# First-batch values moved to SyncE's queue as fp32 and cast by GpSimd; bias factors from a tiny exponential and a bf16 one-hot product; first keys turned ahead of first queries

## The chip, the cores and the metric

The kernel runs on one core of one Trainium2 chip. The metric is device time in microseconds (us), median of several executions. A core has five engines that run their own instruction lists in order and wait for each other by semaphores: TensorE (PE; its weight loads are listed apart as PEld), VectorE (DVE), ScalarE (ACT), GpSimd (POOL) and SyncE (SP). Transfers are issued from SP, ACT or POOL, each with a queue of its own, and all queues are served by the same 16 DMA engines.

## The reference

```python
def _attn_ref(q, k, v, bias_table):            # q, k, v: [8, 8, 576, 64]; bias_table: [32, 8]
    scores = scale * np.matmul(q, k.transpose(0, 1, 3, 2))
    n = np.abs(pos[:, None] - pos[None, :])
    bucket = np.where(n < 16, n, large)         # large: log-spaced buckets 16..31, 31 from distance 128 on
    scores = scores + bias_table[bucket].transpose(2, 0, 1)[None]
    attn = softmax(scores)                      # max taken off, divided by the sum
    return np.matmul(attn, v)

def _moe_ref(x, w1, w2, w3, w_out):             # x: [4608, 512]; d_ff = 768
    h = np.maximum(np.maximum(x @ w1, x @ w2), x @ w3)
    return h @ w_out
```

The attention's output for all 8 batches and 8 heads, laid out as 4608 tokens of 512 columns, is the input of the second function.

## The kernel before

The batches are worked one after the other, each in four **head pairs** (`hp` 0 to 3). Scores are kept turned (keys on partitions), so that `e = exp(scale * scores)` on ACT is already the left operand of the product with the values. The value tile `vx` carries a column of ones after the 64 columns of each head, so the product `a` gives the sum of the exponentials too; `quotients` on DVE divides by it and writes `x_sb`. TensorE turns `x_sb` into `xT`, and the feed-forward products on `xT` (`ps`, later `psp`, `pso`) are fitted between the attention products of the next batch.

The bias is not added but multiplied: DVE multiplies `e` by factors exp(bias - bias of the last bucket). Only a band near the diagonal differs from 1. `spread_bias` makes the factors by distance: a one-hot table `pick` (buckets by distances, built on DVE from a GpSimd iota) times the bias table gives `spread`; ACT turns it into the row `w_sb`, which is written to DRAM (`w_dr`), and SP reads it back shifted by one element per partition as `hank` (`load_hank`). `bandt`, two GpSimd copies of parts of `hank`, is the band for the last 64 keys; `times_bandt` on DVE needs it, and the second half of each first-batch `attend` product needs what `times_bandt` writes.

Of 576 positions, 512 are four tiles of 128 (`KT`), and 64 are a tail with tiles of its own (`qtail`, `ktail`, `vt`), two heads side by side with zeros or ones written by `constants`.

The **order** on each engine is that of the code, as nearly all instructions go through `inorder`. The head of the program, which the change touches, runs so:

- Keys and the first queries of batch 0 are read as fp32 on the queues of ACT and SP into parts of `xT` that are not yet in use (`k32`, `q32`), and cast to bf16 on DVE and ACT (`cast_keys`, `act_copy`). The other queries, the tails and all first values are read by GpSimd's queue, which casts on the way: `vx[0]` by eight transfers of a head each (L306).
- TensorE works nine products on zeros (`warm`) until there is input, then `spread`, then `first_transposes(0)`: queries, then keys, which DVE copies out as `qT` and `kT`.
- A first loop over the head pairs makes half of the scores and exponentials of batch 0 (`visit`), turning the next pair's queries and keys beside it. Then `load_second()` is written, and a second loop makes the other half and the products with the values.
- GpSimd's list goes on, behind the value transfers, with the first weight `w_bf` (L1066, `load_w(0)`), and then with what `load_second` issues: first two heads of batch 1's keys and queries (L247), their tails, the second weight (`load_w(1)`), the two `bandt` copies (L356), the other heads, casts (`spread_packed(0)`), batch 1's values and the third weight.

Of the kernel before, what the change touches and what calls it, by code (L numbers as in the profile page):

```python
# [10 lines left out]
F32 = mybir.dt.float32  # L11
# [28 lines left out]
def kernel(  # L40
# [84 lines left out]
    def dve_copy(out_, in_):  # L125
        return inorder(nc.vector.tensor_copy(out_, in_))
# [7 lines left out]
    def constants(i):  # L134
        inorder(nc.vector.memset(ktail[i][:], 0.0))
        if i == 0:
            inorder(nc.vector.memset(qtail[i][64:, :, :], 0.0))
        inorder(nc.vector.memset(vt[i][:], 0.0))
        inorder(nc.vector.memset(vx[i][:, :, :, D:AW], 1.0))
        for par in range(2):  # L140
            inorder(nc.vector.memset(vt[i][64 * par : 64 * par + 64, :, par, D:AW], 1.0))
# [88 lines left out]
    def borrow(c, n):  # L230
        return xT[:, c, NTOK - 2 * n :].bitcast(F32)

    k32 = borrow(3, KT * H * D).rearrange("p (t h d) -> p t h d", t=KT, h=H)
    q32 = borrow(2, 2 * KT * D).rearrange("p (t h d) -> p t h d", t=2, h=KT)

    def load_32(src, h, dst, eng, nt=KT):
        inorder(eng.dma_start(out=dst[:, :, h, :], in_=main_part(src, 0)[:, 0:nt, h, :]))
# [22 lines left out]
    table = stage.tile([NB, H], F32, name="table")  # L260
    nc.gpsimd.dma_start(out=table[:], in_=bias_table)
    ident = const.tile([P, P], BF16, name="ident")
    make_identity(nc, ident[:])
    load_32(k, 0, k32, nc.scalar)
    load_32(k, 1, k32, nc.scalar)
    for h in range(2, KT):
        load_32(q, h, q32, nc.scalar, 2)
    nc.scalar.preload_act_table_set("natural_log_exp_and_others")
    for h in range(2):
        load_32(q, h, q32, nc.sync, 2)  # L270
    for h in range(2, H):
        load_32(k, h, k32, nc.sync)
# [6 lines left out]
    nc.gpsimd.iota(ids[:, 0:NW], pattern=[[1, NW]], base=0, channel_multiplier=0)  # L279
    nc.gpsimd.iota(ids[:, NW:], pattern=[[0, 1]], base=0, channel_multiplier=1)  # L280
    pick = xT[0:NB, 1, spare].bitcast(F32)
    zeros = xT[:, 1, NTOK - CH :]
    inorder(nc.vector.memset(zeros, 0.0))
    constants(0)
    inorder(nc.vector.memset(qtail[1][64:, :, :], 0.0))
    dve_copy(pick[:], ids[:])
    ranges = _bucket_ranges(S, NB, 128)
# [8 lines left out]
    inorder(nc.vector.tensor_scalar(
        out=pick[:, 0:NW], in0=pick[:, 0:NW], scalar1=pick[:, NW:], scalar2=None, op0=ALU.is_equal,
    ))
    constants(1)
    load_main(q, 0, KT, H, batch[0][0], 0, 2)  # L300
    load_tail(k, 0, 0, H, k_diag)
    load_main(q, 0, 0, H, batch[0][0], 2, KT)
    load_q_tail(0)
    load_tail(v, 0, 0, H, v_diag)
    for h in range(H):
        in_turn(0, nc.gpsimd.dma_start(out=vx[0][:, :, h, 0:D], in_=main_part(v, 0)[:, :, h, :]))  # L306
# [13 lines left out]
    on_zeros(warm[:, 0:CH], 9)  # L320

    act_copy(batch[0][0][:, 0:2, 0:2, :], q32[:, :, 0:2, :])
    w_sb = stage.tile([H, WL], BF16, name="w_sb")

    def spread_bias():
        spread = ps_a.tile([H, NW], F32, tag="a", name="spread")
        mm(spread[:], lhsT=table[:], rhs=pick[:, 0:NW])
        negc = stage.tile([H, 1], F32, name="negc")
        inorder(nc.vector.tensor_scalar(
            out=negc[:], in0=spread[:, HALF:], scalar1=-1.0, scalar2=None, op0=ALU.mult,  # L330
        ))
        for out_, in_ in ((w_sb[:, HALF:], spread[:]), (w_sb[:, 0:HALF], spread[:, HALF:0:-1])):
            inorder(nc.scalar.activation(out=out_, in_=in_, func=ACTF.Exp, bias=negc[:]))
        inorder(nc.scalar.dma_start(out=w_dr[:], in_=w_sb[:]))
# [413 lines left out]
    def first_transposes(hp):  # L748


        hs = slice(2 * hp, 2 * hp + 2)
        tp = ps_f.tile([P, 2 * CH], BF16, tag="ff", name="tp1")
        K, L = KT * P, KT * P + P
        tq = tp[:, L:] if hp else ps_f.tile([P, 2 * CH], BF16, tag="ff", name="tq1")
        for t in range(2):
            tr(tq[:, P * t : P * t + P], batch[0][0][:, t, hs, :].rearrange("p h d -> p (h d)"), ident[:])
        for t in range(KT):
            tr(tp[:, P * t : P * t + P], batch[0][1][:, t, hs, :].rearrange("p h d -> p (h d)"), ident[:])
        e = K if hp < 2 else L
        if e > K:  # L760
            tr(tp[:, K:L], ktail[0][:, hp, :], ident[:])
        dve_copy(qk[0][0][:, hp, 0:QS], tq[:, 0:QS])
        dve_copy(qk[0][1][:, hp, 0:e], tp[:, 0:e])
# [304 lines left out]
    load_w(0)  # L1068
    batch[1] = load_tiles()
# [30 lines left out]
    for hp in range(HP):  # L1100
# [330 lines left out]
```

## Time and profile before

| | |
|---|---|
| time, median of 3 runs (lowest, highest) | 307.15 us (306.98, 308.83) |
| span of the profiled execution, first to last instruction | 305.2 us |
| what the median has more than this span | 1.95 us |
| busy PE / PEld / DVE / ACT / POOL | 295.5 / 183.7 / 206.3 / 201.3 / 143.7 us |
| DMA | 40.51 MB, mean 133 GB/s |

The profiled execution's own device time is not listed, only its span; 1.95 us is taken for what lies around a span. All starts below are in us from the span's start. A row of the timeline has the start, the busy time of the merged instructions, engine and line, what is written and read with shapes, the count, and in brackets the idle time of that engine just before and what ended it. `SPq` and `ACTq` are DMA issues. A row of the chain of waits has start, length and what the end of the program depended on. A row of the DMA issues has the size and the median us from issue to landing.

### The profile page before, as it was taken

The numbers are of one execution on the slowest core, as the hardware profiler recorded it, in microseconds if no ns is written. First come the engines' busy times: TensorE is split into PE (matmuls) and PEld (weight loads), VectorE is DVE, ScalarE is ACT, GpSimd is POOL, SyncE is SP. The second block draws the span as 40 slices with busy tenths as digits, with TensorE's granted clock in tenths as the row PEclk, the third lists the DMA queues.
The fourth block names the chain that finished last, engine by engine and source line by source line (L and its number), as shares of the span: only waits on it lengthen the run. The fifth ranks groups of instructions, "written<-read, shape, count | busy, mean of one in ns | idle before, by whom it ended". The sixth has DMA issues, their size and how long they took to land.

```text
span 305.2 us, 11001 instructions
## 1 busy us (share of the span) xinstructions
PE 295.5 (97%) x4745; PEld 183.7 (60%) x4745; DVE 206.3 (68%) x455; ACT 201.3 (66%) x270; POOL 143.7 (47%) x199
## 2 busy tenths in 40 slices
PE   8789999999999999999999999999999999999995
PEld 2367877765656676567666766676667654444442
DVE  6489888777776677676777677767776765453552
ACT  3999988977786787768776877677777720222211
POOL 8989677725839746774676469462000000000000
PEclk9999999999999999999999999999999999999999
DMA  9999999999999999999999999999623013202003
GB/s 160 187 203 194 176 137 120 114 165 128 223 150 121 150 131 205 174 143 192 181 139 135 202 162 146 138 197 171 79 46 140 6 40 94 84 0 108 31 0 137
DMA packets 165776, 40.51 MB, mean 133 GB/s; under 512 B 154584, under 2 KB 161248, under 8 KB 165728
## 3 DMA queue, kind: packets, MB, share of 16 engines
q0 software_dynamic: 105664, 16.66, 95.5%
q1 hardware_dynamic: 58304, 22.69, 41.6%
q8 instruction: 37, 0.61, 0.8%
q10 hardware_dynamic: 1760, 0.47, 0.7%
q14 instruction: 11, 0.09, 0.1%
HBM read 35.39 MB, written 9.45 MB: 147 GB/s over the span
## 4 chain that ended last, share of the span: by engine, by line
PE 80%; ACT 7%; DMA 6%; DVE 3%; SPq 2%; issue 1%; DVEq 0%; ACTq 0%
PE psp L109 32%; PE ps L109 15%; PE a L109 12%; PE sc L109 8%; PE pso L109 6%; ACT e L827 5%; DMA kT<-ktail 5%; PE sct L109 2%; PE warm L109 1%; PE scq L109 1%; ACT el L827 1%; SPq L738 1%; SPq L731 1%; DVE e L807 1%; DMA out_dram<-osb 1%
## 5 line engine op out<-in xcount | busy, mean ns | idle before, releaser
L827 ACT ACTIVATE e<-sc 128x1024 bf16<-128x1024 f32 x128 | 129.0, 1026 | 29.3 <-PE sc L109 28.0
L109 PEld LDWEIGHTS <-w_bf 64*128 64x128 bf16 (+1 forms) x1112 | 75.8, 95 | 55.3 <-issue 1.9
L109 PE MATMUL psp<-xT,w_bf 64*128 64x512 bf16 x784 | 97.2, 376 | 0.0
L807 DVE TENSOR_TENSOR e<-e,hank 128x512 bf16<-128x512 bf16 (+2 forms) x120 | 56.1, 473 | 13.9 <-ACT e L827 13.2
L109 PE MATMUL ps<-xT,w_bf 128*128 128x512 bf16 (+1 forms) x328 | 59.1, 332 | 0.0
L109 PE MATMUL sc<-qT,kT 64*128 64x256 bf16 (+1 forms) x352 | 48.5, 319 | 2.3 <-ACT e L827 1.1
L109 PEld LDWEIGHTS <-kT 64*128 64x128 bf16 (+1 forms) x712 | 30.0, 94 | 24.8 <-issue 6.8
L109 PE MATMUL a<-vx,e 64*128 64x65 bf16 (+1 forms) x1664 | 44.9, 190 | 0.0
L199 POOL DMA_DIRECT2D k_sb<-in_k_dram x48 | 36.2, 764 | 17.8 <-DMA vx<-in_v_dram 7.8
L199 POOL DMA_DIRECT2D q_sb<-in_q_dram x48 | 36.4, 767 | 15.1 <-DMA vx<-in_v_dram 5.7
L109 PEld LDWEIGHTS <-e 64*128 64x128 bf16 (+1 forms) x1664 | 40.8, 95 | 4.3
L109 PEld LDWEIGHTS <-hT 64*128 64x128 bf16 (+1 forms) x462 | 28.3, 95 | 18.7 <-DVE hT L551 1.6
L167 POOL DMA_DIRECT2D vx<-in_v_dram x28 | 24.8, 893 | 19.5 <-PE a L109 5.4
L109 PE MATMUL psp<-wo_bf,hT 64*128 64x256 bf16 (+1 forms) x360 | 31.7, 305 | 0.0
L421 ACT ACTIVATE m<-ps 128x512 bf16<-128x512 f32 x14 | 8.4, 597 | 34.3 <-PE ps L109 34.3
L827 ACT ACTIVATE el<-sct 128x576 bf16<-128x576 f32 (+2 forms) x36 | 21.7, 605 | 14.0 <-PE sct L109 13.9
L109 PEld LDWEIGHTS <-el 64*128 64x128 bf16 (+1 forms) x676 | 26.4, 94 | 7.0 <-issue 4.4
L109 PE MATMUL a<-vt,el 64*128 64x65 bf16 (+1 forms) x260 | 29.5, 198 | 0.2 <-DVE m L511 0.2
L551 DVE TENSOR_TENSOR hT<-psp,m 128x1024 bf16<-128x1024 f32 (+1 forms) x20 | 18.7, 956 | 9.1 <-PE psp L109 9.1
L109 PE MATMUL pso<-wo_bf,hT 128*128 128x512 bf16 (+2 forms) x102 | 21.7, 366 | 0.0
L430 DVE TENSOR_TENSOR m<-ps,m 128x512 bf16<-128x512 f32 x14 | 9.7, 692 | 17.0 <-PE ps L109 17.0
L537 DVE TENSOR_TENSOR m<-psp,m 128x1024 bf16<-128x1024 f32 x15 | 18.4, 1225 | 3.3 <-PE psp L109 3.1
(82 smaller groups left out, 292.8 us busy)
## 6 DMA issues: line engine op xcount, KB each, us to landing
out_dram<-osb SPq DMA_DIRECT2D x35, 256.0 KB, 4.7
vx<-in_v_dram POOLq DMA_DIRECT2D x28, 128.0 KB, 6.7
q_sb<-in_q_dram POOLq DMA_DIRECT2D x50, 64.0 KB, 5.3
k_sb<-in_k_dram POOLq DMA_DIRECT2D x48, 64.0 KB, 5.3
w_bf<-in_moe_w_dram POOLq DMA_DIRECT2D x2, 512.0 KB, 8.5
xT<-in_k_dram SPq DMA_DIRECT2D x6, 128.0 KB, 4.5
hank<-w_dr SPq DMA_DIRECT2D x2, 384.0 KB, 5.7
w_bf<-in_moe_w_dram POOLq DMA_DIRECT2D x1, 768.0 KB, 8.1
```

The costliest lines, as they stand in the source:

```text
L109: made = inorder(nc.tensor.matmul(*args, **kw))
L167: in_turn(b, nc.gpsimd.dma_start(out=dst[:, t, h0:h1, :], in_=x[:, t, h0:h1, :]), P * (h1 - h0))
L199: in_turn(b, nc.gpsimd.dma_start(out=dst[:, g, :, par, :], in_=part), KT * P)
L421: nc.scalar.activation(out=st[fb]["m0"][:], in_=ps0, func=ACTF.Copy)
L430: inorder(nc.vector.tensor_tensor(out=m[:], in0=ps1, in1=st[fb]["m0"][:], op=ALU.max))
L537: return lambda: inorder(nc.vector.tensor_tensor(out=m[0][:], in0=ps1(), in1=m[0][:], op=ALU.max,))
L551: inorder(nc.vector.tensor_tensor(out=out_[:, i : i + n], in0=ps2()[:, i : i + n], in1=m[0][:, i : i + n], op=ALU.max,))
L731: inorder(nc.sync.dma_start_transpose(out=made[j][:, g, 0 : KT * P].rearrange("p (t n) -> p t n", t=KT), in_=batch[b][j][:, g].rearrange(" ...
L738: inorder(nc.sync.dma_start_transpose(out=made[j][:, :, KT * P : KT * P + n], in_=(qtail, ktail)[j][b % 2][0:n].rearrange("p h c -> p (h c)"),
L807: put(nc.vector.tensor_tensor(out=e4[:, t, :, lo:hi], in0=e4[:, t, :, lo:hi], in1=hank[:, 2 * hp : 2 * hp + 2, c0:c1][:, :, ::-1], op=ALU. ...
L827: made = nc.scalar.activation(out=out_, in_=in_, func=ACTF.Exp, scale=inv_sqrt_d)
```

## The change

- **Bias factors.** Instead of `spread` in fp32 followed by two exponentials with a bias `negc` over 8 x 256 and 8 x 255, the table is read twice (the second time the row of the last bucket on all 32 partitions, by ACT's queue), DVE takes the difference `less` (32 x 8), ACT makes its exponential `factor` in bf16 (32 x 8), TensorE multiplies with a bf16 one-hot `pick`, and ACT copies the product into `w_sb` twice.
- **Head of the program.** Head 0 of the keys goes to SP's queue; `q32` holds two heads instead of four, and heads 2 and 3 of the first queries come by GpSimd's queue with the others. The iotas stand ahead of all GpSimd transfers. Six products on zeros instead of nine. `constants(1)` is moved into the first loop. `first_transposes(0)` turns keys first, then `spread`, then queries.
- **Values.** `vx[0]` is read as fp32 on SP's queue into `v32` (a part of `xT` not yet in use), two heads ahead of the two `hank` transfers and six behind them, and cast by GpSimd in four instructions (`cast_values`), the first ahead of `load_w(0)`, three behind it.

```diff
     def constants(i):
-        inorder(nc.vector.memset(ktail[i][:], 0.0))
-        if i == 0:
-            inorder(nc.vector.memset(qtail[i][64:, :, :], 0.0))
+        if i:
+            inorder(nc.vector.memset(ktail[i][:], 0.0))
+        inorder(nc.vector.memset(qtail[i][64:, :, :], 0.0))
...
-    q32 = borrow(2, 2 * KT * D).rearrange("p (t h d) -> p t h d", t=2, h=KT)
+    q32 = borrow(2, 4 * D).rearrange("p (t h d) -> p t h d", t=2, h=2)
...
-    table = stage.tile([NB, H], F32, name="table")
-    nc.gpsimd.dma_start(out=table[:], in_=bias_table)
-    ident = const.tile([P, P], BF16, name="ident")
-    make_identity(nc, ident[:])
-    load_32(k, 0, k32, nc.scalar)
+    ranges = _bucket_ranges(S, NB, 128)
+    far = next(i for i, r in enumerate(ranges) if r and r[0] <= HALF < r[1])
+    table = stage.tile([NB, 2, H], F32, name="table")
+    load_32(k, 0, k32, nc.sync)
     load_32(k, 1, k32, nc.scalar)
-    for h in range(2, KT):
-        load_32(q, h, q32, nc.scalar, 2)
-    nc.scalar.preload_act_table_set("natural_log_exp_and_others")
+    last_row = bass.AP(tensor=bias_table.tensor, offset=bias_table.offset + far * H, ap=[[0, NB], [1, H]])
+    inorder(nc.scalar.dma_start(out=table[:, 0, :], in_=bias_table))
+    inorder(nc.scalar.dma_start(out=table[:, 1, :], in_=last_row))
     for h in range(2):
         load_32(q, h, q32, nc.sync, 2)
+    nc.scalar.preload_act_table_set("natural_log_exp_and_others")
     for h in range(2, H):
         load_32(k, h, k32, nc.sync)
...
+    load_main(q, 0, 2, H, batch[0][0], 0, 2)
+    ident = const.tile([P, P], BF16, name="ident")
+    make_identity(nc, ident[:])
+    bucket = xT[0:NB, 1, spare].bitcast(F32)
+    pick = xT[0:NB, 2, 0:NW]
...
-    constants(1)
-    load_main(q, 0, KT, H, batch[0][0], 0, 2)
+    constants(0)
+    less = stage.tile([NB, H], F32, name="less")
     load_tail(k, 0, 0, H, k_diag)
+    load_tail(v, 0, 0, H, v_diag)
     load_main(q, 0, 0, H, batch[0][0], 2, KT)
     load_q_tail(0)
-    load_tail(v, 0, 0, H, v_diag)
-    for h in range(H):
-        in_turn(0, nc.gpsimd.dma_start(out=vx[0][:, :, h, 0:D], in_=main_part(v, 0)[:, :, h, :]))
+    v32 = borrow(0, KT * H * D).rearrange("p (t h d) -> p t h d", t=KT, h=H)
+
+    def cast_values(hp):
+        h = slice(2 * hp, 2 * hp + 2)
+        inorder(nc.gpsimd.tensor_copy(vx[0][:, :, h, 0:D], v32[:, :, h, :]))
...
-    on_zeros(warm[:, 0:CH], 9)
+    on_zeros(warm[:, 0:CH], 6)
+
+    cast_keys(0)
+    inorder(nc.vector.tensor_tensor(out=less[:], in0=table[:, 0, :], in1=table[:, 1, :], op=ALU.subtract))
+    factor = stage.tile([NB, H], BF16, name="factor")
+    inorder(nc.scalar.activation(out=factor[:], in_=less[:], func=ACTF.Exp))
...
-        mm(spread[:], lhsT=table[:], rhs=pick[:, 0:NW])
-        negc = stage.tile([H, 1], F32, name="negc")
-        inorder(nc.vector.tensor_scalar(
-            out=negc[:], in0=spread[:, HALF:], scalar1=-1.0, scalar2=None, op0=ALU.mult,
-        ))
+        mm(spread[:], lhsT=factor[:], rhs=pick)
         for out_, in_ in ((w_sb[:, HALF:], spread[:]), (w_sb[:, 0:HALF], spread[:, HALF:0:-1])):
-            inorder(nc.scalar.activation(out=out_, in_=in_, func=ACTF.Exp, bias=negc[:]))
+            act_copy(out_, in_)
         inorder(nc.scalar.dma_start(out=w_dr[:], in_=w_sb[:]))
...
+        for step in (queries, keys, put_queries, put_keys) if hp else (keys, spread_bias, queries, put_keys, put_queries):
+            step()
...
-    cast_keys(0)
-    spread_bias()
     first_transposes(0)
     on_zeros(warm[:, 0:CH])
+    cast_keys(1)
+
+    def load_values(h0, h1):
+        for h in range(h0, h1):
+            inorder(nc.sync.dma_start(out=v32[:, :, h, :], in_=main_part(v, 0)[:, :, h, :]))
+
+    load_values(0, 2)
     for h0 in (0, KT):
         load_hank(h0, h0 + KT)
-    dve_copy(batch[0][0][:, 0:2, 2:KT, :], q32[:, :, 2:KT, :])
-    cast_keys(1)
+    load_values(2, H)
+    cast_values(0)
...
     load_w(0)
+    for hp in range(1, HP):
+        cast_values(hp)
...
         if hp + 2 < HP:
             cast_keys(hp + 2)
+        if hp == 0:
+            constants(1)
```

On **GpSimd**, between the last query transfers of batch 0 and the `bandt` copies, this stood before (in the list of instructions, `xT<-in_k_dram` and `xT<-in_q_dram` are batch 1's keys and queries, `qtail_98` and `ktail_100` its tails):

```order
L177 DMA qtail_97<-in_q_dram 64x8x64
L188 DMA vt_95<-in_v_dram 64x4x64 x2
L306 DMA vx_93<-in_v_dram 128x4x64 x8
L1066 DMA w_bf<-in_moe_w_dram 128x4x768
L247 DMA xT<-in_k_dram 128x2x256
L247 DMA xT<-in_q_dram 128x2x256
L177 DMA qtail_98<-in_q_dram 64x8x64
L188 DMA ktail_100<-in_k_dram 64x4x64 x2
L1066 DMA w_bf<-in_moe_w_dram 128x4x256
L1066 DMA w_bf<-in_moe_w_dram 128x4x512
L356 COPY bandt<-hank 64x768 x2
```

and this stands there now:

```order
L177 DMA qtail_97<-in_q_dram 64x8x64
L311 CAST vx_93<-xT 128x4x2x64
L1088 DMA w_bf<-in_moe_w_dram 128x4x768
L311 CAST vx_93<-xT 128x4x2x64 x3
L247 DMA xT<-in_k_dram 128x2x256
L247 DMA xT<-in_q_dram 128x2x256
L177 DMA qtail_98<-in_q_dram 64x8x64
L188 DMA ktail_100<-in_k_dram 64x4x64 x2
L1088 DMA w_bf<-in_moe_w_dram 128x4x256
L1088 DMA w_bf<-in_moe_w_dram 128x4x512
L362 COPY bandt<-hank 64x768 x2
```

Eight issues, which waited for nothing, are gone; four casts stand in the list, each behind the landing of two heads of values on SP's queue, and all of `load_second`, the `bandt` copies too, stands behind the last of them.

On **SP** at the start of the program, before:

```order
L237 DMA xT<-in_q_dram 128x2x64 x2
L237 DMA xT<-in_k_dram 128x4x64 x6
L340 DMA hank<-w_dr 128x4x384 x2
L731 DMA_TRANSPOSE qT<-q_sb 128x4x128
L731 DMA_TRANSPOSE kT<-k_sb 128x4x128
```

and now:

```order
L237 DMA xT<-in_k_dram 128x4x64
L237 DMA xT<-in_q_dram 128x2x64 x2
L237 DMA xT<-in_k_dram 128x4x64 x6
L1076 DMA xT<-in_v_dram 128x4x64 x2
L346 DMA hank<-w_dr 128x4x384 x2
L1076 DMA xT<-in_v_dram 128x4x64 x6
L737 DMA_TRANSPOSE qT<-q_sb 128x4x128
L737 DMA_TRANSPOSE kT<-k_sb 128x4x128
```

Six of the eight value transfers stand behind `hank`, which waits on SP until `w_dr` has been written.

On **ACT** before the first exponentials (`e<-sc`), before:

```order
L237 DMA xT<-in_k_dram 128x4x64 x2
L237 DMA xT<-in_q_dram 128x2x64 x2
L268 ACT_TABLE_LOAD
L123 ACTIVATE q_sb<-xT 128x2x128
L333 ACTIVATE w_sb<-spread,negc 8x256
L333 ACTIVATE w_sb<-spread,negc 8x255
L334 DMA w_dr<-w_sb 8x511
```

and now:

```order
L237 DMA xT<-in_k_dram 128x4x64
L266 DMA table<-in_bias_table_dram 32x8
L267 DMA table<-in_bias_table_dram 32x8
L270 ACT_TABLE_LOAD
L330 ACTIVATE factor<-less 32x8
L123 ACTIVATE q_sb<-xT 128x2x128
L123 ACTIVATE w_sb<-spread 8x256
L123 ACTIVATE w_sb<-spread 8x255
L340 DMA w_dr<-w_sb 8x511
```

The small exponential has come in ahead of the query cast, and the two large ones have become copies.

More of the change, by code (lines that the diff above doesn't have):

```diff
@@ L278 @@
     ids = xT[0:NB, 0, spare].bitcast(mybir.dt.int32)
-    nc.gpsimd.iota(ids[:, 0:NW], pattern=[[1, NW]], base=0, channel_multiplier=0)
-    nc.gpsimd.iota(ids[:, NW:], pattern=[[0, 1]], base=0, channel_multiplier=1)
-    pick = xT[0:NB, 1, spare].bitcast(F32)
+    inorder(nc.gpsimd.iota(ids[:, 0:NW], pattern=[[1, NW]], base=0, channel_multiplier=0))
+    inorder(nc.gpsimd.iota(ids[:, NW:], pattern=[[0, 1]], base=0, channel_multiplier=1))
+    load_main(q, 0, 2, H, batch[0][0], 0, 2)
[3 more added lines that the diff above has]
+    pick = xT[0:NB, 2, 0:NW]
     zeros = xT[:, 1, NTOK - CH :]
     inorder(nc.vector.memset(zeros, 0.0))
[L284 to L287, printed above, removed]
+    inorder(nc.vector.memset(ktail[0][:], 0.0))
+    dve_copy(bucket[:], ids[:])
     single = 0
@@ L294 @@
             assert hi <= P or vv == NB - 1
-            inorder(nc.vector.memset(pick[:, lo : min(hi, NW)], float(vv)))
+            inorder(nc.vector.memset(bucket[:, lo : min(hi, NW)], float(vv)))
     inorder(nc.vector.tensor_scalar(
-        out=pick[:, 0:NW], in0=pick[:, 0:NW], scalar1=pick[:, NW:], scalar2=None, op0=ALU.is_equal,
+        out=pick, in0=bucket[:, 0:NW], scalar1=bucket[:, NW:], scalar2=None, op0=ALU.is_equal,
     ))
-    constants(1)
-    load_main(q, 0, KT, H, batch[0][0], 0, 2)
+    constants(0)
+    less = stage.tile([NB, H], F32, name="less")
     load_tail(k, 0, 0, H, k_diag)
+    load_tail(v, 0, 0, H, v_diag)
     load_main(q, 0, 0, H, batch[0][0], 2, KT)
     load_q_tail(0)
-    load_tail(v, 0, 0, H, v_diag)
-    for h in range(H):
-        in_turn(0, nc.gpsimd.dma_start(out=vx[0][:, :, h, 0:D], in_=main_part(v, 0)[:, :, h, :]))
+    v32 = borrow(0, KT * H * D).rearrange("p (t h d) -> p t h d", t=KT, h=H)
+    def cast_values(hp):
+        h = slice(2 * hp, 2 * hp + 2)
+        inorder(nc.gpsimd.tensor_copy(vx[0][:, :, h, 0:D], v32[:, :, h, :]))
     def cast_keys(hp):
@@ L754, in first_transposes, with queries, keys, put_queries @@
         tq = tp[:, L:] if hp else ps_f.tile([P, 2 * CH], BF16, tag="ff", name="tq1")
[L755 to L758, printed above, removed]
         e = K if hp < 2 else L
[L760 to L763, printed above, removed]
+        def queries():
+            for t in range(2):
+                tr(tq[:, P * t : P * t + P], batch[0][0][:, t, hs, :].rearrange("p h d -> p (h d)"), ident[:])
+        def keys():
+            for t in range(KT):
+                tr(tp[:, P * t : P * t + P], batch[0][1][:, t, hs, :].rearrange("p h d -> p (h d)"), ident[:])
+            if e > K:
+                tr(tp[:, K:L], ktail[0][:, hp, :], ident[:])
+        def put_queries():
+            dve_copy(qk[0][0][:, hp, 0:QS], tq[:, 0:QS])
+        def put_keys():
+            dve_copy(qk[0][1][:, hp, 0:e], tp[:, 0:e])
+        for step in (queries, keys, put_queries, put_keys) if hp else (keys, spread_bias, queries, put_keys, put_queries):
+            step()
     def last_keys():
```

## The prediction

> **What bounds the kernel now.** I read the share of busy time first, then a table by stage, then the chain of waits through the first 32 us, since every edit lies there.
>
> ```profile
> PE 295.5 (97%) x4745; PEld 183.7 (60%) x4745; DVE 206.3 (68%) x455; ACT 201.3 (66%) x270; POOL 143.7 (47%) x199
> 8.00:16.00 8.00, 6.37 (x62) 2.87 (x60) 3.30 (x11) 7.59 (x11) 8.00 (x12) 1.00 1.69 194
> 16.00:24.00 8.00, 6.73 (x129) 4.89 (x126) 6.90 (x19) 7.63 (x13) 6.96 (x11) 1.00 1.60 191
> 24.00:32.00 8.00, 7.82 (x129) 6.13 (x126) 7.20 (x22) 7.62 (x15) 7.67 (x11) 1.00 1.44 197
> ```
>
> The last three rows are stages of 8 us: busy PE, PEld, DVE, ACT, POOL, the granted clock, the DMA share and GB/s. From 8 to 24 us ACT is full and PE is not. From 24 us on PE is full (7.82 of 8), and over the whole span it is busy 97%: nothing behind 24 us has room to win back what is lost ahead of it, and what is won ahead of it stays won, unless a wait there eats it. The DMA engines are never without work in these stages, and POOL has hardly an idle moment: it is the engine of the list of transfers.
>
> ```profile
> 7.81 1.95 ACT e L827 x2
> 12.65 1.83 ACT e L827 x2
> 22.34 0.60 PE a L109 x18
> 26.67 1.00 PE a L109 x27
> 27.67 0.87 PE ps L109 x8
> ```
>
> So says the chain of waits (its rows between 5 and 32 us, five of them): exponentials from 7.81 us, then products with the values, then the first feed-forward products. No DMA stands in this piece of it. The question is whether the change puts one there.
>
> **The head: what it gains.**
>
> ```profile
> 1.29 0.66 POOL L261 DMA_DIRECT2D table<-in_bias_table_dram  x1 [0.85 <-POOLq L1415]
> 1.19 4.02 PE L109 MATMUL warm<-xT 128*128 128x512 bf16 x9 [1.19 <-DVE xT L283]
> 2.92 0.28 DVE L126 CAST xT<-xT 32x257 f32<-32x257 int32 x1 [0.22 <-POOL xT L280]
> 3.72 0.34 DVE L296 TENSOR_SCALAR xT<-xT 32x256 f32<-32x256 f32 x1
> 4.21 0.42 ACT L123 ACTIVATE q_sb<-xT 128x256 bf16<-128x256 f32 x1
> 4.93 0.43 DVE L126 CAST k_sb<-xT 128x512 bf16<-128x512 f32 x1
> 5.14 1.02 PE L109 MATMUL spread<-xT,table 32*8 32x256 f32 x2
> 6.38 0.82 ACT L333 ACTIVATE w_sb<-spread,negc 8x256 bf16<-8x256 f32 x2 [1.75 <-DVE negc L329]
> 7.23 0.53 ACTq L334 DMA_DIRECT2D w_dr<-w_sb  x1
> 7.81 3.77 ACT L827 ACTIVATE e<-sc 128x1024 bf16<-128x1024 f32 x4 [0.61 <-PE sc L109]
> ```
>
> The one-hot table waits for GpSimd's iota. It loses the transfer of 0.66 ahead of it and `ident`'s two instructions between; I put its end about 1.0 earlier (at least 0.66), so the int cast starts near 1.88 instead of 2.92. From that cast to the end of the comparison are 1.14 us (2.92 to 4.06), then `constants(0)`, 0.9 us of memsets that stood ahead of it before. The first key cast so starts near 3.95 instead of 4.93 and ends at 4.4. The difference `less` behind it is priced like the smallest DVE rows, 0.15; the small exponential has no row (bounds 0.1 and 0.47, the larger being half the `w_sb` row); I take 0.3, ending near 4.9. ACT then works in a line: query cast 0.42, the two copies into `w_sb` 0.82 (bounds 0.6 and 0.9 for copies in place of exponentials), the issue 0.53. That ends at 6.8, and the first `e` starts near 6.85 instead of 7.81: **1.0 us earlier**, 0.5 if the second table transfer lands late. PE keeps up: its product on `factor` is one bf16 pass in place of the 1.02 us in fp32, the two query turns and their copy end near 6.05, scores near 6.7. The nine products take 4.02 us, six take 2.7, so they end at 3.9, ahead of the keys: nothing waits for them. `w_dr` goes out near 6.3 instead of 7.23. `constants(1)`, 0.9 us, now stands in the first loop where DVE is busy 3.30 of 8 us: hidden; uncovered it would cost 0.9. Heads 2 and 3 of the queries arrive by GpSimd's queue instead of ACT's; if they come late for the second pair's turn, up to 0.5 of the 1.0 goes.
>
> **The values: what they do to GpSimd's list.**
>
> ```profile
> 9.42 5.96 POOL L306 DMA_DIRECT2D vx<-in_v_dram  x8
> 16.04 0.77 POOL L247 DMA_DIRECT2D xT<-in_k_dram  x1
> 17.53 0.71 POOL L247 DMA_DIRECT2D xT<-in_q_dram  x1 [0.72 <-DMA vx<-in_v_dram]
> 18.27 0.70 POOL L177 DMA_DIRECT2D qtail<-in_q_dram  x1
> 18.96 1.25 POOL L188 DMA_DIRECT2D ktail<-in_k_dram  x2
> 20.18 1.52 POOL L1066 DMA_DIRECT2D w_bf<-in_moe_w_dram  x2
> 21.67 1.79 POOL L356 COPY bandt<-hank 64x768 bf16<-64x768 bf16 x2
> 25.47 0.89 POOL L252 COPY q_sb<-xT 128x512 bf16<-128x512 bf16 x1
> 23.92 0.25 DVE L907 TENSOR_TENSOR el<-el,bandt 128x192 bf16<-128x192 bf16 x1
> 24.25 0.22 PE L109 MATMUL a<-vt,el 128*128 128x130 bf16 x1
> ```
>
> Before, GpSimd only issues; it passes the values at 15.3 us although they have not landed, and `bandt` is ready at 23.46, 0.46 us ahead of the DVE product that reads it, behind which PE goes on at 24.25. Taking out 5.96 us of issues looks like a gain. But what stands in their place waits for landings, and all of `load_second` waits behind it. Call L the landing of the last value transfer. After it GpSimd does the last cast (0.8: no fp32 cast of this size is in the trace; two bf16 copies of it took 0.89 and 0.64, and 1.8 would be the two `bandt` copies), the same seven issues (0.77, and 4.14 from 17.53 to 21.67: 4.9), `bandt` (1.8), and 0.3 more bring DVE and PE to the place of 24.25. PE resumes there at L + 7.8, so the change costs **L - 16.45**, whatever the head has won. This wait stands on DVE, in front of all its later work: quotients, and so `x_sb`, its turns and the feed-forward products; ACT stops when its score banks are full. All that comes later is moved as a whole.
>
> **When the last value lands.**
>
> ```profile
> xT<-in_k_dram SPq DMA_DIRECT2D x6, 128.0 KB, 4.5
> hank<-w_dr SPq DMA_DIRECT2D x2, 384.0 KB, 5.7
> w_bf<-in_moe_w_dram POOLq DMA_DIRECT2D x1, 768.0 KB, 8.1
> SPq L340 <- DMA w_dr<-w_sb: 5.0, 1, 5.0
> 10.81 0.92 SPq L340 DMA_DIRECT2D hank<-w_dr  x2
> 2.50:5.00 2.50, 2.50 (x7) 0.70 (x5) 2.03 (x25) 1.70 (x2) 2.50 (x7) 1.00 1.17 244
> 17.00:17.75 0.75, 0.04 (x2) 0.06 (x1) 0.75 (x3) 0.75 (x2) 0.22 (x1) 1.00 2.36 157
> 19.50:21.50 2.00, 2.00 (x46) 1.58 (x45) 1.97 (x5) 1.88 (x3) 2.00 (x4) 1.00 1.16 209
> ```
>
> Three rows of issues (KB, us to landing), SP's wait for `w_dr`, the `hank` issue, and three stretches whose last number is GB/s: fp32 reads of batch 0, value reads alone, and the first weight nearly alone. `hank` went out 3.58 us after `w_dr` (7.23 to 10.81); from 6.3 that gives 9.9, and its second half lands near 10.3 + 5.7 = 16.0. SP issues the six values from 10.8 to 13.8, behind it on one queue. Values 0 and 1 go out by 6.7 and land near 11 (4.5), the first cast ends at 12, and the first weight is issued then, on the other queue, so it is in service before value 2. What is left at 16.0 is the weight, 786 KB at 209 GB/s = 3.8 us, and six values of 131 KB at 244 = 3.2 us. If the queues share, the last value is the last of this list: L = 16.0 + 7.0 = **23.0**, and the cost is **6.55 us**. Bounds: if SP's queue were served first, `hank`'s second half would land 5.0 (the shorter of its two) after 10.3, and the values 3.2 behind it: L = 18.5, cost 2.1. At the other end, the whole list ended before with the weight at 15.3 + 8.1 = 23.4; eight values now take 4.3 us at 244 GB/s instead of 3.3 (64 KB each at 157), so L = 24.4, cost 8.0.
>
> Do the queues share? `hank` and the values beside it say so:
>
> ```profile
> DMA to landing us min/median/max: 3.2/4.3/5.4
> DMA to landing us min/median/max: 5.4/5.9/6.3
> DMA to landing us min/median/max: 5.0/5.7/6.4
> ```
>
> These are values 0 and 1 (issued 9.42 and 10.16), values 1 and 2 (10.16 and 10.90), and the halves of `hank` (10.81, and about 0.4 later). Value 0, ahead of `hank`, took 3.2; value 1 landed at 15.5, with `hank`'s first half at 15.8, and value 2 at 17.2, its second half at 17.6 (6.4): one small transfer per large one, both slowed. The Trainium skill, "DMA: Bandwidth & Descriptors", section "Queues, rings and completion order", has each DMA engine take turns between queues packet by packet; by that rule the weight's few large pieces go out among the first values and the last value ends the list, as in the forecast, and the trace agrees (15.5 against 15.8). Strict order by queue would give the 2.1 us instead.
>
> The sum against the profiled execution: 305.2 + 6.55 = 311.7 us of span; with the median's 1.95 us more, **313.7 us**. The head's 1.0 us and the fewer products on zeros do not enter: they end in front of the wait.
>
> **Rivals.**
>
> *SP's queue gets ahead of the weight* (L from 18.5 to 21): cost 2.1 to 4.6, time 309.2 to 311.7. For it: GpSimd's transfers start later after their issue. Against: the pairs just shown.
>
> *GpSimd gets through in time.* The wait decides from L = 16.45 on; if the values land ahead of that, the head's gain is kept, 307.15 - 1.0 = 306.2, and the 5.96 us of issues that are gone may bring batch 1's loads forward. For it: GpSimd's list was 0.46 us ahead of DVE with the eight issues in it. Against: value 7 is issued only at 13.3, behind 786 KB of `hank`; this needs a landing within 3.1 us, the best value landing of before (3.2, with nothing large beside it).
>
> *TensorE slows down in the wait.* At the start, after standing still, nine 512-column products took 4.02 us, 0.45 each; `ps` in the chain takes 0.87 for eight of 256 columns, 0.22 per 512. So PE starts at half pace, for 4 us and more. If a stop of 6 us behind 24 us brings it back there, 4 to 5 us at half pace cost 2.0 to 2.5 where PE is full: 315.7 to 316.2. Against: between 8 us and the end the trace shows no slow pace, nor a stop of this length. The Trainium skill, "TensorE: Matmul & The Clock Gate", section "What's actually happening", says that the clock falls to half after an idle window of about 3.4 us and needs a busy one to return; by that rule this rival holds once the wait is over 3.4 us, and no trace here shows a fall.
>
> *The change does nothing where it counts*: the head's gain and a late `bandt` of a us cancel, within 1%.
>
> **How the numbers follow.** The forecast (shared queues, cost 5.5 to 7.5) 0.38; with the slow restart (7.5 to 10) 0.22; SP's queue ahead 0.20; within 1% or so by cancelling 0.09; in time, with the head's gain, 0.11. The likeliest gives 313.7. The first three make 0.80, from 309.0 to 317.2; about 1% (3 us) is what a measurement of this kernel can tell from no change. Slower by over that: 0.38 + 0.22 and most of SP's queue ahead, 0.72. Within: 0.22, among them most of the case in time, whose gain is only 1.0. Faster by over 1%: 0.06, if batch 1's earlier loads also pay.
>
> **What would show it.** Head: first `e` on ACT near 6.85. Values: GpSimd idle before the second cast until near 20 us, before the last until 23, on value landings; `bandt` near 29 to 31 instead of 21.67; on DVE an idle time of some 6 us before the `bandt` product, released by POOL; PE idle just before the product that follows it. I am wrong if the casts end by 16.5, if the weight lands well behind the values, or if DVE does not wait for `bandt`.

## The result and the profile after

| | before | after |
|---|---|---|
| time, median (lowest, highest), same chip | 307.34 us (306.98, 308.83), 4 runs | 316.48 us (316.05, 318.09), 4 runs |
| ratio, 95% interval | | 1.0286 (1.024 to 1.0332) |
| span of the profiled execution | 305.2 us | 315.1 us |

The change makes the kernel 9.1 us slower: slower as forecast, inside the range, and 2.8 us above the predicted 313.7. The share of busy time and the granted clock over the whole span, of the kernel after:

```profile
PE 298.9 (95%) x4741; PEld 185.7 (59%) x4741; DVE 205.1 (65%) x454; ACT 201.2 (64%) x271; POOL 139.5 (44%) x194
PEclk9999699999999999999999999999999999999999
```

PE is busy 3.4 us longer, for fewer products: part of them ran at a lower clock, which the fifth slice of the clock's row (6) shows, from 31.5 to 39.4 us. GpSimd has 4.2 us less to do than before, and this bought nothing.

The same stages of 8 us as before, of the kernel after (start:end, length, busy PE, PEld, DVE, ACT, POOL, granted clock, DMA share, GB/s):

```profile
24.00:32.00 8.00, 2.06 (x38) 1.32 (x36) 0.91 (x3) 2.72 (x5) 7.12 (x11) 0.93 0.77 77
32.00:40.00 8.00, 7.62 (x94) 5.82 (x95) 6.39 (x19) 4.82 (x10) 7.96 (x11) 0.65 1.48 190
40.00:48.00 8.00, 8.00 (x135) 6.67 (x134) 6.12 (x18) 7.54 (x15) 6.16 (x9) 1.00 1.86 178
```

From 24 to 32 us PE worked 2.06 us where it had worked 7.82 before: a hole. From 32 to 40 us it is busy again, but at a clock of 0.65, and gets through 94 products; one stage later it does 135 in the same time at full clock.

Who waited in the hole is told by the timelines. GpSimd, VectorE and TensorE of the kernel after:

```profile
15.09 0.61 POOL L311 CAST vx<-xT 128x512 bf16<-128x512 f32 x1 [6.43 <-DMA xT<-in_v_dram]
15.64 0.77 POOL L1088 DMA_DIRECT2D w_bf<-in_moe_w_dram  x1
18.60 0.71 POOL L311 CAST vx<-xT 128x512 bf16<-128x512 f32 x1 [2.19 <-DMA xT<-in_v_dram]
24.82 0.61 POOL L311 CAST vx<-xT 128x512 bf16<-128x512 f32 x1 [4.72 <-DMA xT<-in_v_dram]
30.20 1.78 POOL L362 COPY bandt<-hank 64x768 bf16<-64x768 bf16 x2
32.01 0.26 DVE L924 TENSOR_TENSOR el<-el,bandt 128x192 bf16<-128x192 bf16 x1 [7.10 <-POOL bandt L362]
32.33 0.29 PE L109 MATMUL a<-vt,el 128*128 128x130 bf16 x1 [4.82 <-DVE el L924]
```

Read from the bottom: PE stood still 4.82 us for the banded product; DVE stood still 7.10 us for `bandt`; the `bandt` copies start at 30.20 instead of 21.67, since GpSimd's list in front of them waited four times for values, the last time until 24.82. The product at 32.33 stood at 24.25 before: 8.08 us later. TensorE had already waited 1.46 us, until 25.48, for the last cast itself, since the products of the fourth head pair read those values; `bandt` was needed behind them.

The chain of waits of the kernel after carries it through SP's queue (start, length, what was waited for):

```profile
6.74 4.36 DMA w_dr<-w_sb
11.11 0.37 SPq L346
...
12.08 0.72 SPq L1076
...
17.15 7.55 DMA xT<-in_v_dram
...
25.42 1.41 POOL xT L247 x2
...
30.26 0.84 POOL bandt L362
31.15 0.83 POOL bandt L362
32.01 0.27 DVE el L924
32.33 1.28 PE a L109 x18
```

A transfer now stands in the piece of the chain where there was none: the last value, issued at 17.15, in which 7.55 us of waiting lie. In the prediction's terms it lands at L = 24.70.

Whether anything is lost or won later shows in the same exponential far apart. The pair that starts at 42.02 us after and at 32.06 before, and one near the end:

```profile
42.02 1.94 ACT L844 ACTIVATE e<-sc 128x1024 bf16<-128x1024 f32 x2 [0.44 <-PE sc L109]
253.03 1.02 ACT L844 ACTIVATE e<-sc 128x1024 bf16<-128x1024 f32 x1 [0.53 <-PE sc L109]
32.06 1.94 ACT L827 ACTIVATE e<-sc 128x1024 bf16<-128x1024 f32 x2 [0.44 <-PE sc L109]
243.11 1.03 ACT L827 ACTIVATE e<-sc 128x1024 bf16<-128x1024 f32 x1 [0.54 <-PE sc L109]
```

The first two rows are of after, the others of before. The distance is 9.96 us at the one place and 9.92 at the other, and the spans differ by 9.9. All of the loss arises ahead of 42 us, 8.1 in the wait and 1.9 between 32 and 42 us, and is then handed on.

### The profile page after: what moved, and what is told of

Read it like the earlier page. It is cut to its first block, busy times and chain, and to the rows that moved or that the text cites. A ratio compares the mean times of both kernels' runs of the same rounds, so it can differ in the third digit from the quotient of the medians.

```text
span 315.1 us, 10997 instructions
## 1 busy us (share of the span) xinstructions
PE 298.9 (95%) x4741; PEld 185.7 (59%) x4741; DVE 205.1 (65%) x454; ACT 201.2 (64%) x271; POOL 139.5 (44%) x194
## 4 chain that ended last, share of the span: by engine, by line
PE 82%; DMA 5%; ACT 4%; DVE 2%; POOL 2%; SPq 2%; issue 1%; ACTq 0%; POOLq 0%; DVEq 0%
PE psp L109 35%; PE ps L109 16%; PE a L109 13%; PE sc L109 8%; PE pso L109 6%; DMA xT<-in_v_dram 2%; PE sct L109 2%; ACT e L844 2%; SPq L1076 2%; DMA w_dr<-w_sb 1%; PE scq L109 1%; DMA table<-in_bias_table_dram 1%; ACT el L844 1%; DMA out_dram<-osb 1%; POOL bandt L362 1%
## 5 line engine op out<-in xcount | busy, mean ns | idle before, releaser
L109 PE MATMUL sc<-qT,kT 64*128 64x256 bf16 (+1 forms) x352 | 49.4, 329 | 1.2 <-ACT e L844 0.6
L109 PEld LDWEIGHTS <-e 64*128 64x128 bf16 (+1 forms) x1664 | 41.5, 95 | 5.8 <-issue 1.6
L109 PEld LDWEIGHTS <-el 64*128 64x128 bf16 (+1 forms) x676 | 27.1, 95 | 13.0 <-issue 5.4
L167 POOL DMA_DIRECT2D vx<-in_v_dram x28 | 24.8, 892 | 17.4 <-DMA vx<-in_v_dram 9.7
```

Of the source, the lines that this page charges most:

```text
L109: made = inorder(nc.tensor.matmul(*args, **kw))
L167: in_turn(b, nc.gpsimd.dma_start(out=dst[:, t, h0:h1, :], in_=x[:, t, h0:h1, :]), P * (h1 - h0))
```

## Experiments

All times are medians, with lowest and highest run in brackets. The kernel before ran on the same chip in each group: 307.19, 307.11 and 307.21 us in the three groups. Ratios are to these. They lie within 0.23 us of the 307.34 above, so a median is also compared with the changed kernel's 316.48 where the difference is much larger than that.

### One half of the change at a time

`head_alone` has the new bias factors and the new head, with the values by GpSimd's queue as before:

```diff
-    v32 = borrow(0, KT * H * D).rearrange("p (t h d) -> p t h d", t=KT, h=H)
...
+    for h in range(H):
+        in_turn(0, nc.gpsimd.dma_start(out=vx[0][:, :, h, 0:D], in_=main_part(v, 0)[:, :, h, :]))
...
```

> The changed kernel with its new head (bias factors, keys first, six products on zeros), but the first values read by GpSimd's queue as bf16, as before the change. Theory one (GpSimd's list waits for values and holds back the bandt copies): the wait on DVE ahead of the bandt product is gone, and the time is within 1% of before, 306.5 to 309.5 us, as the head's own gain is small. Rival (the head itself costs most, as the second pair's keys and the clock came late in it): 312 us or more.

Measured 309.16 us (308.38 to 310.06), ratio 1.0061 (1.0037 to 1.0085). `values_alone` is the kernel before with only the values changed (fp32 on SP's queue, four casts):

```diff
-    for h in range(H):
-        in_turn(0, nc.gpsimd.dma_start(out=vx[0][:, :, h, 0:D], in_=main_part(v, 0)[:, :, h, :]))
...
+    load_values(0, 2)
     for h0 in (0, KT):
         load_hank(h0, h0 + KT)
+    load_values(2, H)
...
```

> The kernel before with the values alone changed: fp32 on SP's queue, two heads ahead of hank and six behind, four GpSimd casts around the first weight. Theory one: nearly all of the loss is here, 314.5 to 317 us, bandt product on DVE at 31 to 33 us. Rival (the head costs most): 307 to 310 us.

Measured 315.84 us (314.69 to 317.33), ratio 1.0274 (1.021 to 1.0337). The wait is the same one, 5.2 us on DVE here. A row of its timeline and one of its waits (engine, line, what was waited for, us in total, times, longest):

```profile
23.19 0.61 POOL L309 CAST vx<-xT 128x512 bf16<-128x512 f32 x1 [4.74 <-DMA xT<-in_v_dram]
DVE el L910 <- POOL bandt L359: 5.2, 1, 5.2
```

So the values cost 8.6 us by themselves and the head 2.0; together they would give 10.6 where 9.1 were measured, so the two losses don't add by some 1.5 us. The head, which I had down for 1.0 us of gain, is a small loss. What became of its gain comes further down.

### What GpSimd's list has in front of the band

`casts_behind_bandt` takes the last three casts out of the way: they stand behind the `bandt` copies.

```diff
     load_w(0)
-    for hp in range(1, HP):
-        cast_values(hp)
...
                 make_bandt()
+                for hp in range(1, HP):
+                    cast_values(hp)
```

> The changed kernel with the three later value casts moved behind the two bandt copies in GpSimd's list; every transfer, its queue and its order on SP stay. Theory one: bandt is ready near 23, the products with the values wait instead for the casts (last one near 25.5 us), and the time falls to 309.5 to 312 us. Rival (the value traffic on SP's queue is what costs, wherever GpSimd waits for it): 315 to 317 us, as in the changed kernel.

Measured 312.37 us (311.92 to 313.23), ratio 1.0161 (1.0095 to 1.0227). The best of all orders with the new values, 4.1 us less than the changed kernel. GpSimd of this kernel, and the wait of TensorE:

```profile
21.86 1.82 POOL L362 COPY bandt<-hank 64x768 bf16<-64x768 bf16 x2
23.74 1.17 POOL L311 CAST vx<-xT 128x512 bf16<-128x512 f32 x2
27.81 0.61 POOL L311 CAST vx<-xT 128x512 bf16<-128x512 f32 x1 [2.90 <-DMA xT<-in_v_dram]
24.40 0.60 PE L109 MATMUL a<-vx,e 128*128 128x65 bf16 x8 [2.66 <-POOL vx L311]
```

`bandt` is back at its old time (21.67 before), so it was the landings in front of it that delayed it and not the copies. The time did not come back whole: TensorE now waits 2.66 us for the second cast, which waits for nothing but the `bandt` copies in front of it, and TensorE's clock was down behind this wait too (the last section has the row). The last value lands later still (27.7), presumably as more transfers stand beside it, but its cast is done by 28.4, just ahead of the first product that reads it (28.66). An order with the second and third cast ahead of `bandt` and only the last behind it wasn't tried. The expected 312 was missed by 0.4.

`weight_behind_casts` keeps the casts in front, and moves the first weight's transfer behind them, so that it can't stand beside the values:

```diff
-    load_w(0)
     for hp in range(1, HP):
         cast_values(hp)
+    load_w(0)
```

> The changed kernel with the first weight's transfer issued behind the last value cast instead of ahead of the second. Theory one with shared queues: values 6 and 7 no longer stand behind the weight's pieces and land near 19 instead of 24.3 and 24.7, bandt is ready near 27, the time is 309.5 to 312.5 us, and the weight lands near 25, in time for its first product. Rival (the last values are late because SP issues them late and hank is slow): they land at 23 or later and the time stays over 314 us.

Measured 314.28 us (313.33 to 316.83), ratio 1.0233 (1.0163 to 1.0304). Two rows of GpSimd:

```profile
21.67 0.61 POOL L311 CAST vx<-xT 128x512 bf16<-128x512 f32 x1 [1.56 <-DMA xT<-in_v_dram]
27.75 1.79 POOL L362 COPY bandt<-hank 64x768 bf16<-64x768 bf16 x2
```

The last cast starts 3.15 us earlier than in the changed kernel (24.82), so the weight did hold the last values. `bandt` starts 2.45 us earlier only: the weight's own issue, 0.77 us, now stands behind the last cast. The time is 2.2 us less. I had expected 309.5 to 312.5, with landings near 19: I had left out that issue and SP's slow issue of the last two values. The gain may be larger than it looks: the trace of this kernel has a wait of 1.65 us for turned keys at 119.69 us, like the one that comes up below for the head.

### What holds the last values beside the weight

In the changed kernel the value issued just ahead of the weight (at 14.94) landed 4.4 us later; the one issued just behind it (15.93) took 8.3, and so did the weight itself (15.64). These are the rows for these single issues of the changed kernel, in this order (us to landing last), and below them the one for a value that was issued at 15.65 in `weight_behind_casts`, with no weight beside it:

```profile
xT<-in_v_dram SPq DMA_DIRECT2D x1, 128.0 KB, 4.4
DMA to landing us min/median/max: 8.3/8.3/8.3
w_bf<-in_moe_w_dram POOLq DMA_DIRECT2D x1, 768.0 KB, 8.3
DMA to landing us min/median/max: 4.2/4.2/4.2
```

So it is the weight, and not the place on SP's queue, that makes 8.3 us of 4.2. Is it the size of the weight's pieces (its writes are of 1536 bytes)? `weight_in_thirds` loads it as three transfers:

```diff
-        for f0, f1 in ((0, QS), (QS, d_ff)) if i else ((0, d_ff),):
+        for f0, f1 in ((0, QS), (QS, d_ff)) if i else ((0, QS), (QS, 2 * QS), (2 * QS, d_ff)):
```

> The changed kernel with the first weight loaded as three transfers of 256 columns instead of one of 768. Theory 1: each of the weight's pieces, written in 1536 bytes, holds a DMA engine long enough to keep SyncE's values out; at 512 bytes the queues share better, values 6 and 7 land 1 to 2 us before the weight's end, and the last cast ends by 24 us instead of 25.4. The two more issues on GpSimd (0.7 us each) stand ahead of the last three casts, which wait anyway: 314.5 to 316. Rival: what holds the values is the weight's amount, not the size of its pieces: values 6 and 7 land after 24 us as before, and the time is 316 to 318.

Measured 316.47 us (315.44 to 317.68), ratio 1.0283 (1.0246 to 1.0321): no change. The last cast of this kernel:

```profile
25.26 0.61 POOL L311 CAST vx<-xT 128x512 bf16<-128x512 f32 x1 [5.05 <-DMA xT<-in_v_dram]
```

It starts 0.44 us later than with the whole weight (24.82). Smaller pieces don't help; the rival, the amount in front, fits. How a DMA engine chooses between the queues meanwhile isn't settled by this.

`values_ahead` attacks L from the other end: all eight values ahead of `hank` on SP's queue.

```diff
-    load_values(0, 2)
+    load_values(0, H)
     for h0 in (0, KT):
         load_hank(h0, h0 + KT)
-    load_values(2, H)
```

> The changed kernel with all eight value transfers on SyncE's queue ahead of the two band transfers, instead of two ahead and six behind. Theory 1: the price is set by the landing of the last value, which SyncE's late issue (12 to 17.7 us, behind the bias factors) puts behind the weight of 15.6 us; issued from 7 to 13 us the last value lands between 17 and 20 us, the last cast ends by 21, the banded copies run 4 to 5 us earlier, from 25 to 28 us, and the time is 310.5 to 313. Rival: the band transfers, now issued behind the values near 13 to 14 us, come too late and take the last value's place: they land after 21 us and the time stays over 314.

Measured 315.35 us (313.37 to 316.37), ratio 1.0247 (1.0203 to 1.0291). GpSimd of this kernel, and its issues between 14.9 and 16.5 us (KB, us to landing):

```profile
17.88 0.61 POOL L311 CAST vx<-xT 128x512 bf16<-128x512 f32 x1 [0.28 <-DMA xT<-in_v_dram]
27.10 2.22 POOL L362 COPY bandt<-hank 64x768 bf16<-64x768 bf16 x2 [3.81 <-DMA hank<-w_dr]
w_bf<-in_moe_w_dram POOLq DMA_DIRECT2D x1, 768.0 KB, 7.1
hank<-w_dr SPq DMA_DIRECT2D x2, 384.0 KB, 9.1
```

The values came as expected: the last cast ends at 18.5 instead of 25.4. But now the two `hank` transfers, issued at 16.0 and 16.5 behind the weight (15.05), take 9.1 us in the median of the two, and `bandt` waits for them until 27.10. As the rival said, they land after 21 us and the time stays over 314, but it had them late behind the values' issues, which end at 14.7. What held `hank` until 16.0 was a side effect: the row of factors was sent to DRAM at 11.13 instead of 6.74 us, because that transfer signals on the same semaphore as an earlier key transfer, which landed at 11.05; the row itself landed at 16.02. ACT's first exponential, behind it in the list, started at 11.69 instead of 7.39. So this run doesn't show what the order alone would give.

### The slow clock after the wait

`zeros_in_wait` gives TensorE 21 products on zeros ahead of the product that waits. Nothing reads their product:

```diff
+        if hp == 2:
+            on_zeros(ps_f.tile([P, CH], F32, tag="ff", name="busy")[:], 21)
```

> The changed kernel with 21 products on zeros of 128x512 ahead of the product that waits for the first banded exponentials, so that TensorE isn't idle from 26 to 32 us. Theory 1: the 6.8 us at half clock after the wait cost time; with TensorE kept busy the granted clock in 32 to 40 us goes from 0.65 to near 1.0, and the time from 316.5 to 313.5 to 315.3. Rival: in these microseconds ScalarE sets the pace, and half clock costs nothing: the clock rises as said, the time stays at 316 to 317. Second rival: the zeros themselves run past the wait's end and take what they save: same time, and the next product starts after 33 us.

Measured 315.12 us (313.38 to 315.88), ratio 1.0235 (1.0198 to 1.0273), 1.4 us less than the changed kernel. TensorE of this kernel in the wait, the stage behind it, and the exponential that was quoted above:

```profile
26.89 4.71 PE L109 MATMUL busy<-xT 128*128 128x512 bf16 x21
32.14 0.23 PE L109 MATMUL a<-vt,el 128*128 128x130 bf16 x1 [0.25 <-DVE el L924]
32.00:40.00 8.00, 7.76 (x121) 5.95 (x122) 7.33 (x22) 6.47 (x14) 7.96 (x11) 1.00 1.52 191
39.85 1.94 ACT L844 ACTIVATE e<-sc 128x1024 bf16<-128x1024 f32 x2 [0.44 <-PE sc L109]
```

The wait ends at the same place (32.14 against 32.33), so the zeros took nothing; the clock is 1.00 instead of 0.65, and 121 products instead of 94 are done in this stage. The exponential of 42.02 comes at 39.85. In these two traces the slow clock so costs 2.0 us (42.02 - 39.85, less the 0.19 by which the wait ended earlier), in the medians 1.4. The intervals of the two ratios overlap a little (1.0286 from 1.024, 1.0235 to 1.0273), so it is mainly the traces, one of each kernel, that speak against the rival by which it costs nothing.

### Where the head's gain went

The first exponential of `head_alone` is early (6.92, 0.9 us ahead of before), but the second pair's comes late, at 10.39 instead of 9.63, and its queue of keys and its clock both look guilty: the keys of heads 2 and 3 landed at 6.2 and 7.7 us instead of 5.5 and 6.5, and the eight scores took 1.0 us instead of 0.6. Three kernels built on `head_alone` try this. `head_nine` gives nine products on zeros again:

```diff
-    on_zeros(warm[:, 0:CH], 6)
+    on_zeros(warm[:, 0:CH], 9)
```

> head_alone (the new bias factors and key order, values as before) with nine products on zeros instead of six ahead of the first real ones. Theory 1: head_alone's loss of 1.9 us comes from the clock that is granted late (12.7 us against 6.2 before), for lack of steady work on TensorE: full clock comes by 8 to 9 us, the scores of the second pair take 0.6 instead of 1.0 us, and the time is 307 to 308.5. Rival: the loss comes from the keys of heads 2 and 3, which land late: the time stays at 309 to 309.5.

Measured 308.34 us (307.31 to 311.47), ratio 1.0028 (1.0001 to 1.0056). `head_keys_act` starts the keys of heads 2 and 3 on ACT's queue:

```diff
+    for h in range(2, KT):
+        load_32(k, h, k32, nc.scalar)
...
-    for h in range(2, H):
+    for h in range(KT, H):
         load_32(k, h, k32, nc.sync)
```

> head_alone with the keys of heads 2 and 3 started on ScalarE's queue behind the tables, not on SyncE's behind the first keys and queries. Theory 1: the late landing of these keys (6.2 and 7.7 us against 5.5 and 6.5 before) holds the second pair: they land 1 us earlier, the second pair's exponential starts near 9.3 instead of 10.4, and the time is 307.3 to 308.5. Rival: GpSimd's large query transfer takes the DMA engines wherever the keys are queued, or the clock's late grant sets the second pair: same start within 0.3 us and 309 to 309.5.

Measured 309.73 us (308.9 to 310.26), ratio 1.0072 (1.0049 to 1.0095). `head_both` has both edits:

> head_alone with both edits: nine products on zeros, and the keys of heads 2 and 3 on ScalarE's queue. Theory 1: if both causes add, the head keeps its earlier first exponential and loses nothing behind it: 306 to 307, at or below the kernel before. Rival: one cause is all of it, and the other edit adds nothing: the same time as the better of the two single edits. Second rival: the head's loss has another cause (the work on VectorE that now stands ahead of the casts): 309 again.

Measured 309.43 us (308.38 to 310.38), ratio 1.0068 (1.0044 to 1.0092). The second pair's scores in `head_alone` and in `head_nine`:

```profile
9.74 1.04 PE L109 MATMUL sc<-qT,kT 64*128 64x256 bf16 x8
9.60 0.61 PE L109 MATMUL sc<-qT,kT 64*128 64x256 bf16 x8 [0.28 <-DVE kT L126]
```

Nine zeros give back the pace: in the trace's clock records full clock is first granted at 5.7 us in `head_nine` (6.2 before), and at 12.7 in `head_alone` (13.8 in the changed kernel). That part of the theory holds. It is worth 0.35 us at the second pair (10.04 against 10.39), and 0.8 in the medians, whose intervals overlap; the rest of the loss stays. The keys moved to ACT's queue came later, not earlier: the cast that waits for them starts at 9.28 instead of 7.75, and the second pair at 11.89. That theory is out.

`head_split_q` takes the remaining suspect: in `head_nine`, GpSimd's first query transfers are cut, heads 2 and 3 first, heads 4 to 7 behind the identity.

```diff
-    load_main(q, 0, 2, H, batch[0][0], 0, 2)
+    load_main(q, 0, 2, KT, batch[0][0], 0, 2)
     ident = const.tile([P, P], BF16, name="ident")
     make_identity(nc, ident[:])
...
+    load_main(q, 0, KT, H, batch[0][0], 0, 2)
     load_tail(k, 0, 0, H, k_diag)
```

> head_nine with GpSimd's first query transfers (heads 2 to 7, 1.4 us) cut in two: heads 2 and 3 at the same place, heads 4 to 7 behind the identity. Theory 1: the six-head transfers, started 1.4 us earlier than in the kernel before, take the DMA engines from the keys of heads 2 and 3; with a third of them in front these keys land near 5.6 and 6.6 us instead of 6.7 and 7.9, the second pair's exponential starts by 9.4 instead of 10.0, and the time is 306.8 to 308. Rival: the two further issues on GpSimd (0.8 us each) push back its later transfers, values and weight, and take as much as the keys gain: 308 to 309.

Measured 309.26 us (307.84 to 312.77), ratio 1.0062 (1.0032 to 1.0093): no gain. ACT and a late wait of PE in this kernel, and the same wait of `head_alone` behind them:

```profile
7.20 3.77 ACT L842 ACTIVATE e<-sc 128x1024 bf16<-128x1024 f32 x4 [0.59 <-PE sc L109]
12.96 1.95 ACT L842 ACTIVATE e<-sc 128x1024 bf16<-128x1024 f32 x2
114.07 0.39 PE L109 MATMUL sc<-qT,kT 64*128 64x512 bf16 x2 [1.73 <-DMA kT<-k_sb]
114.25 0.39 PE L109 MATMUL sc<-qT,kT 64*128 64x512 bf16 x2 [1.92 <-DMA kT<-k_sb]
```

The head does now what was wanted: four exponentials in one piece from 7.20, as before from 7.81. So GpSimd's large query transfer was what held the second pair's keys. Yet the third pair's exponentials come at 12.96 instead of 12.53, the next transfers having been put back, and a wait of 1.7 to 1.9 us stands at 114 us, a hundred microseconds on, on the turned keys of a later batch. That wait is in the traces of `head_alone`, `head_nine` (3.2 us) and `head_split_q`, and not in those of before, `head_keys_act`, `head_both` or the changed kernel. `weight_behind_casts` has it too. Each is the trace of one execution, and those of `head_alone` (310.06 us) and `head_nine` (311.47) are the slowest of their kernels, so how often the wait comes isn't known. In the trace of `head_alone` the exponential that starts at 32.06 before starts at 33.51, 1.45 us late, and the span is 3.1 us longer; the rest arises later, most of it at this wait. Why these keys come late there wasn't tried; about half of the head's loss is open so far. None of these kernels beats the kernel before, and no order of the values came near it.

## Why the prediction was right, and where it was off

**The mechanism** held at each step named beforehand: casts that wait for landings, the second at 18.6 (forecast near 20), the last at 24.8 (23), `bandt` at 30.2 (29 to 31), DVE idle 7.10 us for it (some 6), PE idle just before the product behind. `casts_behind_bandt` showed that it is these waits in front of `bandt` that delay it.

**The formula** cost = L - 16.45 was good: with the landing of the trace, 24.70, it gives 8.25, and PE resumed 8.08 later.

**L was the term that was mis-sized**, 23.0 forecast and 24.70 measured. I had built it as `hank`'s landing at 16.0 plus 7.0 us for the rest of the list. `hank`'s second half landed at 17.3: the factors went out at 6.74 instead of 6.3, and SP got on 4.36 us later instead of 3.58, so 1.3 of the 1.7 us lie in front of the last six values. The list itself took 7.4 instead of 7.0. Two details of it were wrong and cancelled out: the first two values, for which the first cast waits, landed at 14.0 and 15.0, not near 11, so that the weight was issued at 15.64, not 12, behind values 2 to 5; and SP issued the last six values until 17.65 instead of 13.8, at up to 1.18 us each, so that two of them fell behind the weight.

```profile
12.08 5.57 SPq L1076 DMA_DIRECT2D xT<-in_v_dram  x6
```

The upper bound, 24.4, should have been the working value: it started from the end that the same list of transfers had in the trace of before (23.4), where the forecast added up rates behind an estimated start.

**TensorE's slow pace** was a rival with 0.22, and it was so; left out of the forecast's sum, it is at least half of the miss of 2.8 us: 1.9 us in the trace, 1.4 in the medians by `zeros_in_wait`, against 2.0 to 2.5 put down for it. With L at 24.7 and 1.9 for the clock, the sum is 305.2 + 8.25 + 1.9 = 315.35 us of span, beside the 315.1 of the trace; the median has 1.4 us more than this span, where 1.95 had been added. So the forecast was inside its range because its bounds were wide enough for two misses on the same side; its working value had no term for the clock. The Trainium skill, "TensorE: Matmul & The Clock Gate", section "What's actually happening", gives about 3.4 us of idling to the fall; here the clock fell in a wait of 4.82 us, and `zeros_in_wait`, which filled it, kept full clock. In `casts_behind_bandt` it was down around a wait of only 2.66 us, so the trace of that run doesn't agree with 3.4. I had weighed that rule by "no trace here shows a fall", when no trace could: in the kernel before no wait of TensorE behind 8 us is over 0.8 us.

**The head's 1.0 us**: the first exponential came 0.42 us earlier instead of 1.0 in the changed kernel, 0.9 in `head_alone`. What went in the changed kernel is the 0.5 that I had put down for a late table: `less`, forecast behind the first key cast at 4.4, waited for it until 5.21.

```profile
5.21 0.15 DVE L328 TENSOR_TENSOR less<-table 32x8 f32<-32x8 f32 x1 [0.67 <-DMA table<-in_bias_table_dram]
```

(The bound of 0.47 for the small exponential was no half of the row of 0.82, which is 0.41; it took 0.21.) The larger error of the head is the next step: I took a first exponential that is early for a head that is early. The second pair hangs on other keys, which GpSimd's query transfers, now ahead of the identity, delayed, as `head_split_q` shows. I had bounded this by 0.5 of lost gain; in `head_alone` the second pair was 0.76 us behind its old start (10.39 against 9.63), in the changed kernel 1.37 (11.00). In the sum it was rightly left out, since it ends in front of the wait.

**The rivals**: SP's queue ahead of the weight is refuted by the 4.4 and 8.3 us on either side of the weight's issue; the one in which GpSimd gets through in time, by L. That the queues share is how I argued for 23.0; the pair of rows 4.4 and 8.3 says rather that what SP issues behind the weight waits for most of it, though the weight is on GpSimd's queue.

## What to carry to other kernels

An engine that issues transfers in order is cheap only while it issues: a cast in its list makes each landing a gate for all that stands behind, so ask what that is and whether it is needed sooner than the data waited for. Price a hole on TensorE with the clock behind it; products on zeros in the hole won that part back here (1.4 us). A head that delivers its first tile earlier was worth nothing by itself here: look at the second and third, and at what the earlier transfers push back.

## What the runs showed of the hardware that I had not expected

The slow pace after an idle TensorE outlasts the wait by several microseconds: 0.65 of full clock on the mean from 32 to 40 us, 94 products against 121.

How long it must stand idle isn't settled. From 22 to 24 us of `casts_behind_bandt`, inside a wait of 2.66 us with waits of 0.25 and 0.80 us shortly ahead of it, the clock was 0.50 (first row below).

At the start, the number of products on zeros goes with the time at which the clock comes. The kernels with nine (before, `values_alone`, `head_nine`, `head_split_q`, `head_both`) have their first grant of full clock at 4.7 to 6.2 us, and six of the eight with six (after, `head_alone`, `head_keys_act`, `values_ahead`, `casts_behind_bandt`, `weight_behind_casts`) at 12.7 to 19.4 us. The other two, `zeros_in_wait` and `weight_in_thirds`, have it at 4.2 and 4.9 us, so with six it differs from trace to trace, and with one execution of each kernel the three products aren't shown to be the cause. What is granted can be lost again in the head: it was in these two and in `head_both` (mean of 0.57 from 8 to 16 us). The second row is of `zeros_in_wait`:

```profile
22.00:24.00 2.00, 0.00 (x0) 0.00 (x0) 0.94 (x2) 0.70 (x1) 1.88 (x3) 0.50 1.24 191
8.00:16.00 8.00, 7.38 (x48) 3.44 (x49) 4.22 (x16) 5.56 (x9) 2.14 (x4) 0.60 1.59 225
```

The column of the granted clock doesn't show a late first grant: it has 1.00 from 8 to 16 us in `head_alone`, whose first grant is at 12.7. There the duration of like products is the better witness, 1.04 us in `head_alone` against 0.61 in `head_nine`.

SP's issues are not of one length: in the changed kernel about 0.5 us each for the first three transfers, and 0.72 to 1.18 for five of the last six values, which are all of one size, though the sixth took 0.51 again. Why isn't shown.
